# A gated linear attention and an MLP in one program: output products of 384 columns, two attention streams, whole padded loads, dummy products and a new order

## The chip, the cores and the metric

One core of one Trainium2 chip runs the program. The metric is device time in microseconds (us), the median of three runs: 546.33 before (545.84 to 546.39). The engines are named as in the profile: PE is TensorE's matmuls, PEld its weight loads, DVE VectorE, ACT ScalarE, POOL GpSimd, SP SyncE, which issues nearly all transfers.

## The reference

Four batches, 8 heads, 768 tokens, head size 48. The attention is a recurrence for each batch and head; its output, 3072 rows of 384, goes through an MLP with weights in float64:

```python
for t in range(S):
    state = alpha[:, :, t, :, None] * state + np.einsum('bhd,bhe->bhde', k[:, :, t], v[:, :, t])
    y[:, :, t] = np.einsum('bhd,bhde->bhe', q[:, :, t], state)
...
h = x @ w_in                                        # 384 -> 2048
sp = np.maximum(h, 0.0) + np.log1p(np.exp(-np.abs(h)))
return ((h * erf(sp)) @ w_out).astype(np.float32)   # 2048 -> 384
```

## The kernel before, in words

**Attention** is done in 24 chunks (class Chunk, line 251). A chunk is 64 tokens of two batches (m is the pair of batches, c the place in time), all 8 heads. la, lk, lq and lv load alpha, k, q and v. sb and sa are two scans of alpha on DVE; rc and ic note an inverse for a check at the end; kk and qq multiply k and q with the scans; pn turns K by PE and kn copies it out; ps makes the scores, mk masks them; qt and sv make the chunk's output in PSUM (py) from the state T and from the scores; pu and ta renew the state, td scales it. xh (ACT) and xl (DVE) split the output into a high and a low part, x_hi and x_lo, in the reduced float32 that PE multiplies fast. Chunks 0 to 11 are the first pair of batches in order of time, 12 to 23 the second.

**The MLP** is done in 12 blocks of 256 tokens (class Moe, line 418), two chunks each, in 4 groups g of 512 hidden units, and a group in two halves. hm (line 471) makes 18 products of 256 columns for a half, over x_hi, x_lo and the weights' parts wi_hi and wi_lo; he copies them out. u, n1, n2, n3, ma, mb, g, z1 and z2 are the activation, by two table sets on ACT: need (line 236) loads a set when the step wants another one than the last. ga and gl split the result into gh and gl; om (line 554) adds 18 products of 256 columns into acc: three blocks of 128 output columns, two of hidden units, three terms, with the weights as the stationary operand and the tokens as the columns. oe copies acc out three times, od sends it, oa on ACT's queue.

**Weights** come as float64, 12 blocks of w_in and 16 of w_out (class Weight, line 584). wl loads, wy, wv, wa and wb make float32 of the bits, wh the high part. The low part is made by wq (a subtraction on DVE) or by wp (two products on PE, with the identity and its negative) and we (a copy by ACT); before, all 12 blocks of w_in use wp and we, all 16 of w_out wq.

**The order** of all steps is a string, ORDER, read once (line 767). Class Queue (line 177) chains each engine's instructions in that order, SP's transfers too, so every engine works strictly through its part of the string. In the end f1, f2 and f3 reduce checks to one number, all engines load it, and a branch skips general (line 653), a slow path for unusual values that is not taken here.

Of the kernel before, what the change touches and what calls it, by code (L numbers as in the profile page):

```python
# [21 lines left out]
RT2 = 2.0**0.5  # L22
# [4 lines left out]
wli_0 wyi_0 wvi_0 wai_0 la_0 sb_0 rc_0 wli_7 wbi_0 whi_0 wpi_0 wli_9 lk_0 sa_0 wyi_7 wvi_7 wai_7 wyi_9 wli_5  # L27
la_1 lq_0 wvi_9 lv_0 wai_9 wli_1 wbi_7 wbi_9 kk_0 pn_0 wvi_5 lk_1 sb_1 whi_9 wpi_9 wyi_5 wai_5 wli_2 whi_7 wei_0
wpi_7 kn_0 qq_0 lv_1 ic_0 rc_1 sa_1 lq_1 la_2 wei_9 pu_0 ta_0 wyi_1 wvi_1 wei_7 wli_8 wyi_2 wli_6 wli_11 wbi_5
wli_3 wlo_0 ps_0 mk_0 sv_0 xh_0 wai_1 kk_1 pn_1 wli_4 wvi_2 wbi_1 wai_2 td_1 whi_5 whi_1 wpi_5 wbi_2 kn_1 wyi_8  # L30
wei_5 xl_0 pu_1 qq_1 ta_1 sb_2 wvi_8 wpi_1 qt_1 ps_1 td_2 wai_8 wvi_6 wbi_8 whi_2 lk_2 wyi_6 wpi_2 wei_1 mk_1
sv_1 wai_6 whi_8 wvi_11 ic_1 wyi_11 wei_2 xh_1 wbi_6 whi_6 wlo_7 wai_11 wvi_3 lq_2 wbi_11 wyi_3 wai_3 wpi_8
wei_8 whi_11 rc_2 ic_2 wpi_6 wei_6 wbi_3 sa_2 wli_10 whi_3 la_3 wyo_0 wpi_11 wei_11 xl_1 wvi_4 wpi_3 wei_3 wvo_0
wyi_4 wyo_7 kk_2 wao_0 wai_4 wvo_7 wbo_0 wlo_3 who_0 hm_0_0_0 he_0_0_0 wbi_4 whi_4 wao_7 wqo_0 pn_2 wbo_7 kn_2
hm_0_0_1 he_0_0_1 qq_2 wpi_4 wvi_10 lv_2 qt_2 sb_3 wyi_10 wai_10 wlo_5 rc_3 wlo_1 ps_2 mk_2 lk_3 wvo_3 wbi_10
wlo_2 wei_4 hm_0_1_0 pu_2 who_7 wqo_7 u_0_0 wyo_3 whi_10 wvo_5 he_0_1_0 wlo_6 sa_3 ta_2 la_4 n1_0_0 wvo_1 wao_3
wyo_5 sv_2 td_3 kk_3 wpi_10 wei_10 wbo_3 hm_0_2_0 wvo_2 who_3 wyo_2 wao_5 hm_0_1_1 pn_3 wyo_1 wqo_3 wao_2 xh_2
wao_1 he_0_2_0 lq_3 xl_2 hm_0_3_0 n2_0_0 wbo_1 n3_0_0 kn_3 lv_3 pu_3 lk_4 who_1 wbo_2 sb_4 ic_3 he_0_1_1 wlo_8
qq_3 qt_3 wbo_5 rc_4 who_2 wqo_1 ta_3 who_5 wqo_5 u_0_1 ma_0_0 g_0_0 he_0_3_0 ps_3 mk_3 td_4 hm_0_2_1 wlo_11
he_0_2_1 sv_3 kk_4 xh_3 wvo_6 n1_0_1 lq_4 sa_4 hm_0_3_1 la_5 xl_3 hm_1_0_0 he_0_3_1 mb_0_0 qq_4 n2_0_1 z1_0_0  # L40
wqo_2 z2_0_0 sb_5 pn_4 ic_4 n3_0_1 ma_0_1 kn_4 wyo_6 wvo_11 wvo_8 wao_6 lk_5 wlo_4 wlo_9 lv_4 ga_0_0_1 gl_0_0_1
hm_1_2_0 ga_0_0_0 qt_4 ps_4 mk_4 wbo_6 he_1_0_0 mb_0_1 he_1_2_0 kk_5 g_0_1 z1_0_1 gl_0_0_0 wyo_8 wao_8 who_6
u_0_2 n1_0_2 z2_0_1 hm_1_2_1 he_1_2_1 wyo_11 wao_11 wqo_6 wbo_8 rc_5 om_0_0_1 hm_1_1_0 he_1_1_0 pu_4 wvo_4
wbo_11 n2_0_2 n3_0_2 wyo_4 sv_4 who_11 ta_4 ma_0_2 wqo_11 om_0_0_0 ga_0_1_1 wao_4 wlo_10 xh_4 who_8 ic_5 td_5
wlo_12 pn_5 kn_5 hm_1_1_1 ga_0_1_0 wbo_4 who_4 wvo_9 wyo_9 mb_0_2 he_1_1_1 wao_9 xl_4 g_0_2 hm_1_0_1 wqo_8
gl_0_1_1 lv_5 hm_1_3_0 wqo_4 lk_6 wlo_13 he_1_0_1 he_1_3_0 om_0_1_1 sa_5 lq_5 wvo_10 wyo_10 hm_1_3_1 u_0_3
n1_0_3 z1_0_2 wao_10 qq_5 qt_5 ps_5 wyo_13 gl_0_1_0 wbo_9 who_9 n2_0_3 n3_0_3 z2_0_2 ga_0_2_0 om_0_1_0 la_6 lv_6
wqo_9 wyo_12 mk_5 ga_0_2_1 wbo_10 who_10 lq_6 sb_6 gl_0_2_0 wvo_13 ma_0_3 wqo_10 sv_5 xh_5 wvo_12 xl_5 g_0_3
wao_13 wao_12 u_1_0 he_1_3_1 wlo_15 gl_0_2_1 wlo_14 rc_6 u_1_1 n1_1_0 pu_5 ta_5 om_0_2_0 wvo_15 mb_0_3 wbo_13
n1_1_1 z1_0_3 wbo_12 hm_2_0_0 he_2_0_0 wyo_15 who_13 td_6 om_0_2_1 z2_0_3 sa_6 hm_2_1_0 he_2_1_0 kk_6 ga_0_3_0  # L50
# [36 lines left out]
xh_14 hm_6_1_0 he_6_1_0 u_5_3 om_5_0_0 sa_15 hm_6_1_1 n1_5_3 ga_5_1_0 n1_6_0 om_5_1_1 z2_5_2 hm_6_3_0 td_15
# [51 lines left out]

@with_exitstack  # L140
def gla_moe(ctx: ExitStack, tc: tile.TileContext, q, k, v, alpha, w_in, w_out, out):
    nc = tc.nc


    M, CPB, _, D, NP, NI, TC = q.shape
    P = NI * TC
    B, H, S = M * NI, 2 * NP, CPB * TC
    W = NP * NI * TC
    DM, NT = out.shape
    FF = w_in.shape[1]  # L150
    TB = 256
# [685 lines left out]
```

## Time and profile before

| | |
|---|---|
| median of 3 runs | 546.33 us |
| the profiled execution, own time | 547.01 us |
| its span, first to last instruction | 545.3 us |
| mean granted clock of TensorE | 0.995 |
| instructions | 18043 |
| PE / ACT / DVE busy | 516.9 / 496.2 / 470.5 us |
| ACT table loads | 64, 82.1 us |

The span is what the profiler sees of one execution; the execution's own time has 1.7 us more around it. "Busy" counts the time in which an engine had an instruction under way; ends of matmuls are modelled and overlap, so the distance of starts, not the length, is what one costs. All steps are recorded at line 185, the helper of class Queue, so the rows are told apart by tiles: `ph` is written by hm, `acc` by om, `py` by qt and sv, `pS` by ps, `rest` by wp, `wbuf` is a weight block being unpacked.

### The profile page before, as it was taken

To read this page: it belongs to the slowest core of one execution; us is meant where nothing else is said; L and a number is where in the kernel's file an instruction comes from. 1 tells how busy PE (TensorE), PEld (TensorE's weight loads), DVE (VectorE), ACT (ScalarE), POOL (GpSimd) and SP (SyncE) were. 2 spreads that over 40 slices of the span, in tenths; PEclk is the share of its full clock that TensorE was granted. 3 is DMA by queue.
4 is the path that set the end of the run, shared out by engine and by line. 5 is a ranking of instruction groups with operands and counts; after the bars stand their busy time and mean duration, and the time that the engine had idled before them with its cause. 6 is when DMAs were issued, how large, how long until landed. Compare 5 with 4: busy or idle time off the path is not lost.

```text
span 545.3 us, 18043 instructions
## 1 busy us (share of the span) xinstructions
PE 516.9 (95%) x7998; PEld 488.4 (90%) x7998; DVE 470.5 (86%) x613; ACT 496.2 (91%) x695; POOL 3.5 (1%) x18
## 2 busy tenths in 40 slices
PE   1799999999999999999999999999999999999984
PEld 0457999999999999999999999999999999999984
DVE  6899999999999999999698899698687887987772
ACT  3579999999999999898999999999899999999981
POOL 2000000000000000000000000000000000000000
PEclk9899999999999999999999999999999999999999
DMA  6967335213021023311022203022020202000001
GB/s 197 304 198 227 108 98 151 94 46 93 15 71 51 15 61 83 87 40 50 17 79 84 60 17 107 17 60 69 17 70 2 73 12 85 1 13 19 30 1 35
DMA packets 38101, 38.98 MB, mean 71 GB/s; under 512 B 22144, under 2 KB 26752, under 8 KB 38016
## 3 DMA queue, kind: packets, MB, share of 16 engines
q1 hardware_dynamic: 37872, 37.63, 23.6%
q8 instruction: 64, 1.05, 0.8%
q14 instruction: 21, 0.17, 0.1%
q10 hardware_dynamic: 144, 0.13, 0.1%
HBM read 33.03 MB, written 4.72 MB: 69 GB/s over the span
## 4 chain that ended last, share of the span: by engine, by line
PE 52%; ACT 35%; DVE 6%; issue 4%; DMA 1%; DVEq 0%; ACTq 0%; SPq 0%
PE ph L185 22%; PE acc L185 20%; ACT s L185 10%; ACT w L185 6%; ACT L185 6%; ACT gh L185 4%; ACT hs L185 4%; PE py L185 3%; PE rest L185 2%; DVE wbuf L185 2%; PE pu L185 2%; PE pS L185 2%; PE pn L185 1%; DMA raw_a<-in_alpha_dram 1%; ACT kn L185 1%
## 5 line engine op out<-in xcount | busy, mean ns | idle before, releaser
L185 PE MATMUL ph<-x_hi,wi_hi 128*128 128x256 f32 x576 | 165.5, 287 | 1.0 <-ACT hs L185 0.9
L185 PE MATMUL acc<-gh,wo_hi 128*128 128x256 f32 x576 | 164.9, 286 | 0.4 <-ACT gh L185 0.3
L185 PE MATMUL acc<-gl,wo_hi 128*128 128x256 f32 x576 | 162.7, 283 | 1.9 <-DVE gl L185 1.7
L185 PE MATMUL ph<-x_lo,wi_hi 128*128 128x256 f32 x576 | 162.0, 281 | 0.2 <-DVE x_lo L185 0.2
L185 PE MATMUL acc<-gh,wo_lo 128*128 128x256 f32 x576 | 161.8, 281 | 0.0
L185 PE MATMUL ph<-x_hi,wi_lo 128*128 128x256 f32 x576 | 161.7, 281 | 0.0
L185 PEld LDWEIGHTS ph<-x_hi,wi_hi 128*128 128x128 f32 x576 | 108.5, 188 | 4.0 <-ACT hs L185 1.6
L185 PEld LDWEIGHTS acc<-gl,wo_hi 128*128 128x128 f32 x576 | 108.5, 188 | 3.6 <-DVE gl L185 3.5
L185 PEld LDWEIGHTS acc<-gh,wo_hi 128*128 128x128 f32 x576 | 108.5, 188 | 2.5 <-ACT gh L185 0.7
L185 PEld LDWEIGHTS ph<-x_lo,wi_hi 128*128 128x128 f32 x576 | 108.6, 188 | 0.5 <-DVE x_lo L185 0.4
L185 PEld LDWEIGHTS acc<-gh,wo_lo 128*128 128x128 f32 x576 | 108.6, 188 | 0.0
L185 PEld LDWEIGHTS ph<-x_hi,wi_lo 128*128 128x128 f32 x576 | 108.5, 188 | 0.0
L185 DVE TENSOR_TENSOR gl<-hs,gh 128x512 fp32r<-128x512 f32 x96 | 65.3, 684 | 30.3 <-ACT gh L185 29.7
L185 ACT ACT_TABLE_LOAD x64 | 82.1, 1283 | 1.9 <-PEq L797 0.8
L185 ACT ACTIVATE gh<-hs 128x512 fp32r<-128x512 f32 x96 | 59.1, 624 | 9.5 <-PE acc L185 4.3
L185 DVE TENSOR_TENSOR t<-s,w 128x1024 f32<-128x1024 f32 x48 | 58.4, 1217 | 9.0 <-ACT w L185 8.7
L185 DVE TENSOR_TENSOR s<-s,w 128x1024 f32<-128x1024 f32 x48 | 58.5, 1219 | 8.9 <-ACT s L185 7.4
L185 DVE SCALAR_TENSOR_TENSOR hs<-s,hs 128x1024 f32<-128x1024 f32 x48 | 58.5, 1220 | 0.8
L185 DVE SCALAR_TENSOR_TENSOR w<-t,w 128x1024 f32<-128x1024 f32 x48 | 58.4, 1218 | 0.6
L185 ACT ACTIVATE hs<-ph 128x512 f32<-128x512 f32 x96 | 55.2, 587 | 1.7 <-PE ph L185 1.5
L185 ACT ACTIVATE s<-s,fixed 128x1024 f32<-128x1024 f32 x48 | 54.8, 1148 | 0.3
L185 ACT ACTIVATE s<-s 128x1024 f32<-128x1024 f32 x48 | 50.3, 1057 | 2.2 <-DVE t L185 1.8
(66 smaller groups left out, 637.9 us busy)
## 6 DMA issues: line engine op xcount, KB each, us to landing
wst<-in_moe_w_in_dram SPq DMA_DIRECT2D x12, 512.0 KB, 6.2
raw_v<-in_v_dram SPq DMA_DIRECT2D x24, 256.0 KB, 3.1
wst<-in_moe_w_out_dram SPq DMA_DIRECT2D x16, 384.0 KB, 4.0
raw_a<-in_alpha_dram SPq DMA_DIRECT2D x48, 96.0 KB, 2.9
raw_k<-in_k_dram SPq DMA_DIRECT2D x48, 96.0 KB, 2.6
raw_q<-in_q_dram SPq DMA_DIRECT2D x48, 96.0 KB, 2.3
out_dram<-o SPq DMA_DIRECT2D x35, 128.0 KB, 2.0
out_dram<-o ACTq DMA_DIRECT2D x1, 128.0 KB, 4.1
```

What stands on the lines that cost most here:

```text
L185: ins = made(*args, **kw)
```

## The change

- **om** takes the tokens as the stationary operand and 384 weight columns as the moving one: 12 products in place of 18. acc is two tiles of 128 tokens x 384. The terms run gh by wo_hi, gh by wo_lo, gl by wo_hi; in the last om of a block all of the first tile's products come first. hm runs x_hi by wi_hi, x_hi by wi_lo, then x_lo. The output is stored by tokens, in two transfers a block (od), without oa.
- **Chunks** alternate between the two pairs of batches (n = 2c + m), each with its own two T tiles. pn, ps, pu and f2 share one PSUM tile `both`, pu in columns 256 to 447 of either bank; a first product fills those columns. kn holds 48 of 64 columns, mask is BF16.
- **Loads** of alpha, k and q: the arrays are padded before the launch to 128 rows (alpha also between its segments), so one transfer brings a whole tile, and the memsets of these tiles go. k and q have two buffers each, and K and Q are formed in place.
- **Six blocks of w_in** (6 to 11) use wq in place of wp and we.
- **Dummy products** dw_n: n products of the identity with itself into acc's second bank, 57 in ten places of the order, 46 of them ahead of the first hm.
- **ORDER** is another. It begins with la_0, sb_0 and wlo_1. The steps u, g and n1, n2, n3 switch tables 59 times in the new string, 63 times in the old one. At the end ic_23 stands after the last om. The branch takes another layout.

The diff, cut to its core; of the order only the beginning and the end are shown:

```diff
-wli_0 wyi_0 wvi_0 wai_0 la_0 sb_0 rc_0 wli_7 wbi_0 whi_0 wpi_0 wli_9 lk_0 sa_0 wyi_7 wvi_7 wai_7 wyi_9 wli_5
+la_0 sb_0 wlo_1 wvo_1 rc_0 wyo_1 wao_1 sa_0 wbo_1 wli_1 wvi_1 wyi_1 who_1 wli_2 wli_5 wvi_2 wai_1 wyi_2 wai_2
+wqo_1 lk_0 wyi_5 wvi_5 wbi_1 whi_1 dw_22 wpi_1 la_1 kk_0 pn_0 wai_5 wbi_2 whi_2 wbi_5 whi_5 wli_0 wyi_0 wvi_0
...
-gl_11_2_0 om_11_2_0 z2_11_3 ga_11_3_1 gl_11_3_1 om_11_3_1 ga_11_3_0 gl_11_3_0 om_11_3_0 oe_11_2 od_11_2 f1 f2 f3
-oe_11_0 oe_11_1 oa_11_1 od_11_0
+z2_11_3 ga_11_3_0 gl_11_3_0 om_11_3_0 ga_11_3_1 gl_11_3_1 om_11_3_1 ic_23 oe_11_0 od_11_0 oe_11_1 f1 od_11_1 f2
+f3
...
-    rq, rk = (raw.tile([P, NP, NI, TC], F32, name=f"raw_{nm}") for nm in "qk")
-    for t, fill in ((ra, 1.0), (ra[:, 0 : 1 + L : SEG], 0.0), (rk, 0.0), (rq, 0.0)):
-        dve.memset(t, fill)
+    rq, rk = ([raw.tile([P, NP, NI, TC], F32, name=f"raw_{nm}{n}") for n in range(2)] for nm in "qk")
...
+    both = ps_at.tile([P, 2, 512], F32, name="both", tag="b")
...
-            self.m, self.c = divmod(n, CPB)
+            self.c, self.m = divmod(n, M)
...
         def lk(self):
-            self.load(rk.rearrange("p a i t -> p (a i) t"), k)
+            self.K = rk.pop(0)
+            rk.append(self.K)
+            sp.dma_start(out=self.K, in_=k[self.m, self.c])
...
         def hm(self, g, half):
-                for kt in range(KT):
-                    for wt, xt in ((wi_hi, x_hi), (wi_hi, x_lo), (wi_lo, x_hi)):
+            for wt, xt in ((wi_hi, x_hi), (wi_lo, x_hi), (wi_hi, x_lo)):
+                for u in range(2):
+                    for kt in range(KT):
...
         def om(self, g, half):
-            for d in range(KT):
-                for u in range(2):
-                    for n, (wt, gt) in enumerate(((wo_hi, gh), (wo_lo, gh), (wo_hi, gl))):
-                        pe.matmul(
-                            out=o, lhsT=wt[:, f, ds], rhs=gt[:, u, :],
...
+            terms = ((gh, wo_hi), (gh, wo_lo), (gl, wo_hi))
+            todo = [(c, u, n) for n in range(3) for c in range(TB // P) for u in range(2)]
+            if end:
+                todo.sort(key=lambda x: x[0])
+            for k, (c, u, n) in enumerate(todo):
+                gt, wt = terms[n]
+                pe.matmul(
+                    out=self.acc[c][:, :DM], lhsT=gt[:, u, c * P : (c + 1) * P], rhs=wt[:, g * GT + half * 2 + u, :],
+                    start=begin and (u, n) == (0, 0), stop=end and not any(c == x for x, *_ in todo[k + 1 :]),
+                )
...
-        def oe(self, d):
-            o = self.pl.gp.tile([P, TB], F32, name="o", tag="o", bufs=3)
+        def oe(self, c):
+            o = self.pl.gp.tile([P, DM], F32, name="o", tag=f"o{c}", bufs=1)
...
+        def dw(self, n):
+            for _ in range(n):
+                pe.matmul(out=self.t[:, :P], lhsT=ident, rhs=ident, start=True, stop=True)
...
-    with tc.If(rv > 0):
+    with tc.If(rv > 0, preferred_fallthrough_block=False):
```

## Rows read from the trace of the kernel before

**Rows 1.** The page's head: span, and each engine's busy time, share and instructions.
```profile
span 545.3 us, 18043 instructions
PE 516.9 (95%) x7998; PEld 488.4 (90%) x7998; DVE 470.5 (86%) x613; ACT 496.2 (91%) x695; POOL 3.5 (1%) x18
```

**Rows 2.** The table by stages: from and to, length, busy time and instructions of PE, PEld, DVE, ACT and POOL, then the granted clock of TensorE, the share of the DMA engines and GB/s.
```profile
20.00:39.28 19.28, 16.05 (x347) 9.09 (x346) 17.85 (x33) 12.80 (x27) 0.00 (x0) 0.91 0.79 252
39.28:100.00 60.72, 59.18 (x1111) 55.29 (x1114) 58.68 (x101) 58.09 (x91) 0.00 (x0) 1.00 0.50 147
100.00:220.00 120.00, 119.06 (x1957) 114.69 (x1945) 115.98 (x148) 118.44 (x166) 0.00 (x0) 1.00 0.20 55
220.00:380.00 160.00, 160.00 (x2511) 155.93 (x2510) 139.04 (x165) 151.99 (x207) 0.00 (x0) 1.00 0.21 57
380.00:500.00 120.00, 119.17 (x1798) 115.39 (x1797) 97.19 (x111) 115.58 (x153) 0.00 (x0) 1.00 0.12 33
500.00:537.80 37.80, 35.94 (x292) 34.59 (x291) 27.87 (x36) 30.28 (x39) 0.00 (x0) 1.00 0.03 11
```

**Rows 3.** The timeline of PE from 300 to 306 us, with one weight load (PEld) of the timeline of all engines: start, length, engine, line, operation and tiles.
```profile
300.47 0.28 PE L185 MATMUL ph<-x_hi,wi_lo 128*128 128x256 f32 x1
300.68 0.86 PE L185 MATMUL py<-Q,T 48*32 48x64 f32 x64
301.47 0.69 PE L185 MATMUL pS<-Q,K 48*64 48x64 f32 x32
302.09 0.39 PE L185 MATMUL acc<-gh,wo_hi 128*128 128x256 f32 x1
302.32 0.28 PE L185 MATMUL acc<-gh,wo_lo 128*128 128x256 f32 x1
302.32 0.19 PEld L185 LDWEIGHTS acc<-gl,wo_hi 128*128 128x128 f32 x1
304.21 0.27 PE L185 MATMUL acc<-gl,wo_hi 128*128 128x256 f32 x1
304.41 0.68 PE L185 MATMUL pu<-raw_v,kn 64*64 64x48 f32 x32
305.03 0.86 PE L185 MATMUL py<-sT,raw_v 64*32 64x64 f32 x64
305.81 0.38 PE L185 MATMUL ph<-x_hi,wi_hi 128*128 128x256 f32 x1
```

**Rows 4.** The timeline of PE ahead of the first product of the MLP; the second line is the second half of the pair in the first, seen in a narrower window.
```profile
36.98 1.02 PE L185 MATMUL rest<-wbuf,ident 128*128 128x512 f32 x2
37.41 0.59 PE L185 MATMUL rest<-wbuf,ident 128*128 128x512 f32 x1
38.07 1.02 PE L185 MATMUL rest<-wbuf,ident 128*128 128x512 f32 x2
39.28 0.39 PE L185 MATMUL ph<-x_hi,wi_hi 128*128 128x256 f32 x1
```

**Rows 5.** DVE up to 39.3 us: its first work on a weight block and its second x_lo in the timeline, and two lines of its waits (who, for whom: us in total, times, longest).
```profile
5.08 0.43 DVE L185 TENSOR_SCALAR wbuf<-wst 128x512 int32<-128x512 int32 x1 [2.38 <-DMA wst<-in_moe_w_in_dram]
38.60 0.53 DVE L185 TENSOR_TENSOR x_lo<-py,x_hi 128x384 fp32r<-128x384 f32 x1
DVE T L185 <- PE pu L185: 2.3, 2, 2.1
DVE B L185 <- DMA raw_a<-in_alpha_dram: 1.3, 1, 1.3
```

**Rows 6.** Groups of ACT's instructions by form, whole span: busy us, mean ns of one, and the idle time before them.
```profile
L185 ACT ACT_TABLE_LOAD x64 | 82.1, 1283 | 1.9 <-PEq L797 0.8
L185 ACT ACTIVATE wi_lo<-rest 128x512 fp32r<-128x512 f32 x12 | 7.1, 594 | 3.0 <-PE rest L185 2.9
L185 ACT ACTIVATE kn<-pn 128x512 f32<-128x512 f32 x22 | 12.9, 586 | 0.6 <-PE pn L185 0.6
L185 ACT ACTIVATE o<-acc 128x256 f32<-128x256 f32 x36 | 12.4, 376 | 4.2 <-PE acc L185 4.2
L185 ACT ACTIVATE x_hi<-py 128x384 fp32r<-128x384 f32 x24 | 11.5, 480 | 3.5 <-PE py L185 3.5
```

**Rows 7.** The end: the last PE product, the copies of acc, the last transfer issued (timelines), the time to landing of the last three output transfers (least, median, most), and two lines of PE's sequencer at the branch (length in ns, first and last start).
```profile
537.49 0.28 PE L185 MATMUL acc<-gl,wo_hi 128*128 128x256 f32 x1
537.81 0.94 ACT L185 ACTIVATE o<-acc 128x256 f32<-128x256 f32 x3 [4.17 <-PE acc L185]
538.77 0.38 ACTq L185 DMA_DIRECT2D out_dram<-o  x1
DMA to landing us min/median/max: 1.7/4.0/4.1
L782 PEldq COMPARE_BRANCH  x1: 4100/4100/4100, 538.7 to 538.7; - x1
L782 PEldq EVENT_SEMAPHORE  x1: 51/51/51, 542.9 to 542.9; - x1
```

**Rows 8.** A load of k in SP's timeline and its use by DVE, and the page's line on such loads (KB each, median us to landing).
```profile
291.79 0.80 SPq L185 DMA_DIRECT2D raw_k<-in_k_dram  x2
299.70 0.69 DVE L185 TENSOR_TENSOR K<-raw_k,B 128x512 f32<-128x512 f32 x1
raw_k<-in_k_dram SPq DMA_DIRECT2D x48, 96.0 KB, 2.6
```

More of the change, by code (lines that the diff above doesn't have):

```diff
@@ L142, in gla_moe @@
     nc = tc.nc
-    M, CPB, _, D, NP, NI, TC = q.shape
-    P = NI * TC
+    M, CPB, P, NP, NI, TC = q.shape
     B, H, S = M * NI, 2 * NP, CPB * TC
     W = NP * NI * TC
-    DM, NT = out.shape
+    NT, DM = out.shape
     FF = w_in.shape[1]
@@ L239, in need @@
             act.preload_act_table_set(name)
-    Ts = [at.tile([P, NI * NP * HD], F32, name="T", tag=f"T{n}", bufs=1) for n in range(2)]
-    for t in Ts:
+    Ts = [[at.tile([P, NI * NP * HD], F32, name="T", tag=f"T{m}{n}", bufs=1) for n in range(2)] for m in range(M)]
+    for t in Ts[0] + Ts[1]:
         nc.gpsimd.memset(t, 0.0)
-    T, Td = Ts
-    Tv, Tdv = (t.rearrange("p (i a d) -> p i a d", i=NI, a=NP)[:, :, :, :D] for t in Ts)
+    Tv = [[t.rearrange("p (i a d) -> p i a d", i=NI, a=NP)[:, :, :, :D] for t in pair] for pair in Ts]
+    both = ps_at.tile([P, 2, 512], F32, name="both", tag="b")
+    pe.matmul(
+        out=both[:, 1, NP * TC : NP * (TC + D)], lhsT=ident, rhs=Ts[0][0][:, : NP * D],
+        start=True, stop=True,
+    )
     PIECES = (((0, 0),), ((1, 16),), ((0, 32), (1, -16)))
@@ L312, in pn @@
                 return
-            self.pn_ = ps_at.tile([P, 2, 512], F32, name="pn", tag="b")
+            self.pn_ = both
             for pair in range(NP):
@@ L321, in kn @@
                 return
-            self.kn_ = at.tile([P, NP, 2, HD], F32, name="kn", tag="kn", bufs=1)
-            act.activation(self.kn_.rearrange("p a b d -> p (a b d)"), self.pn_[:, 0, :], AF.Copy)
+            self.kn_ = at.tile([P, NP, 2, D], F32, name="kn", tag="kn", bufs=1)
+            rows = self.pn_[:, 0, :].rearrange("p (a b d) -> p a b d", a=NP, b=2)
+            act.activation(self.kn_, rows[:, :, :, :D], AF.Copy)
         def td(self):
@@ L389, in pu @@
                 return
-            self.pu_ = ps_at.tile([P, NI, 512], F32, name="pu", tag="b")
+            self.pu_ = both[:, :, NP * TC :]
             for pair in range(NP):
@@ L395, in pu @@
                         pe.matmul(
-                            out=self.pu_[half * HD : (half + 1) * HD, i, pair * D : (pair + 1) * D],
+                            out=self.pu_[half * HD : half * HD + D, i, pair * D : (pair + 1) * D],
                             lhsT=self.kn_[toks, pair, half, :], rhs=self.v[toks, h * HD : h * HD + D],
@@ L658, in general @@
             DG = D // NG4
-            part = dram.tile([NG4, M, CPB, NI, TC, NP, 2, D], F32, name="part")
+            part = dram.tile([NG4, CPB, M, NI, TC, NP, 2, D], F32, name="part")
             rec = es.enter_context(ExitStack())
@@ L727, in general @@
                         m.om(g, half)
-                for d in range(KT):
+                for d in range(2):
                     m.oe(d)
@@ L757, in f2 @@
         def f2(self):
-            self.pf = ps_at.tile([P, 2, 512], F32, name="pf", tag="b")
+            self.pf = both
             pe.matmul(out=self.pf[:1, 0, :1], lhsT=self.good[:, 3:4], rhs=ones, start=True, stop=True)
@@ L765, in gla_moe, with __init__ @@
     flags = Flags()
+    class Warm:
+        def __init__(self):
+            self.t = None
+        def dw(self, n):
+            if self.t is None:
+                self.t = ps_acc.tile([P, 512], F32, name="warm", tag="acc1")
+            for _ in range(n):
+                pe.matmul(out=self.t[:, :P], lhsT=ident, rhs=ident, start=True, stop=True)
+    warm = Warm()
     for name, arg in steps:
@@ L820 @@
             a[..., 1, :] = a[:, :, ::-1, :, :, 1, :].copy()
+            wide = _np.full((M, C, 2, 64, NP, NI, TC), float(name == "alpha"), a.dtype)
+            wide[:, :, :, :D] = a
+            a = wide.reshape(M, C, 128, NP, NI, TC)
+            if name == "alpha":
+                wide = _np.zeros((M, C, 128, 1 + NP * NI * (TC + 1)), a.dtype)
+                wide[..., 1:].reshape(M, C, 128, NP, NI, TC + 1)[..., :TC] = a
+                a = wide
         elif name == "moe_w_in":
```

302 lines of the change are left out of this document (144 added, 158 removed).

## The prediction

> **What bounds the kernel now.** I read the engines' shares first [rows 1]: TensorE (PE) 95%, ScalarE (ACT) 91%, VectorE (DVE) 86%. Three engines that full hide who leads, so the table by stage comes next [rows 2]. From the first product of the MLP at 39.28 us [rows 4] on, PE is busy in nearly all of each stage, ACT in 474.4 of 498.5 us, and DVE in 174.7 of the 180.7 us up to 220 and much less later. But a PE that looks busy need not be dense, so the PE timeline is my price list [rows 3]. Inside a group the starts of two products of 256 columns lie (304.21 - 302.32) / 16 = 0.118 us apart, 2.126 us for 18. A visit to the attention costs 0.79 for qt, 0.62 for ps, 0.62 for pu and 0.78 for sv, plus 0.2 for going and coming back: 0.09 before the first py product and 0.11 because the first acc product takes 0.23. pn is put at 0.43, four times 128 columns at the fp32 rate below.
>
> Now the sum behind the first product: 192 groups x 2.126 = 408.2; 21 qt, 22 ps, 20 pu, 22 sv and 20 pn = 68.4; 63 visits (counted in the order string) x 0.2 = 12.6; one split of a weight block 1.1. That is 490.3 of the 498.3 us from 39.28 to the end of the last product at 537.6 (start 537.49, [rows 7]). So PE's own work sets the end; only 8 us are lost, and a shorter product is worth its whole saving until ACT or DVE take over. Ahead of the first product DVE leads: it does 50 steps (counted in the order string), then x_lo of the second chunk at 38.60; it waits 2.38 us for the first weight block, 1.3 for alpha and 2.3 for PE's pu [rows 5]. PE's granted clock is lowered for part of it (0.91 as the mean of 20 to 39.28 us, 1.00 in every later stage [rows 2]).
>
> **The change part by part.**
> Output products. 18 products of 256 columns per group become 12 of 384: the same 4608 columns, a third fewer instructions. No row shows a slot of 384. At one column a cycle of 2.4 GHz, 256 columns would take 106.7 ns; the rows show 118. Is the rest a price per column, per product, or a weight load that 256 columns just fail to cover? The nearest rows: a 512-column fp32 product starts 36.98, its second half 37.41 [rows 4], 0.43 later, where streaming at two cycles a column is 0.427: hardly anything is added when the stream is long. A weight load starts with each product (302.32 [rows 3]) for the next one, and 384 columns give it 53 ns more time. So I take 160 + 2.3 = 162.3 ns, 1.95 a group, 0.178 saved x 96 = **17.1 us**. Ends: the same 11 ns added (171.4 ns) leaves 6.6 us; scaled by columns (177 ns), nothing.
> The Trainium skill, TensorE: Matmul & The Clock Gate, section Back-to-back issue gap, gives N/2.4 + 2.5 ns for a product alone, at full clock: 109.2 for 256 and 162.5 for 384. By it a group would go from 1.966 to 1.950 and the change of shape would be worth 1.5 us in all; but the rows show 118 for 256, not 109, so the trace does not bear it out where it can be tried.
>
> Order within a group. gl and x_lo come last now: eight of twelve output products and twelve of eighteen input products run without them. Price nothing; it shortens waits that PE hardly has in the middle, and a little in the last 38 us, where 1.9 us of PE stand idle [rows 2].
>
> Attention. PE issues the same products. kn copies 384 columns instead of 512 (0.59 to 0.48 by x_hi, a PSUM copy of 384 [rows 6]), 2.3 us of ACT. T alternates between two sets, which only loosens a chain. pS, pu and pn share one tile with fixed places, so pu need not wait for sT. K and Q are formed in place: at no cost in DVE time, but the load of k now waits for ps and pn of two chunks before (rival three). Behind the first product one pu and one qt more remain: 0.6 + 0.8.
>
> Loads. One issue in place of two for alpha, k and q; four memsets leave DVE at the start, two join POOL, which has nothing to do later. Alpha's load is first on SP's queue, ahead of the weight blocks, and wlo_1 goes ahead of the input blocks. So DVE can scan at about 4 us, where it began with a weight block at 5.08 and then waited 1.3 for alpha [rows 5].
>
> Weights. Six of twelve lower halves go from PE (1.09 us, the distance 36.98 to 38.07 [rows 4]) and ACT (0.59 [rows 6]) to one DVE subtraction. Five of these six PE splits lay ahead of the first product, one (1.1) behind.
>
> Dummies. 57, each two passes of 128 columns of fp32: 2 x 0.107 = 0.215 (a quarter of 0.43). 46 stand ahead of the first product, in PE's waits there; if these waits are shorter than thought they delay it, at most 46 x 0.215 = 9.9, at half clock twice that. 11 stand behind it: 2.4 us, paid in full where PE is dense.
>
> First product. DVE does 50 steps ahead of the second x_lo in both. Off go the later start (1.1), part of the waits for the load (1.0) and for a slow pu (1.0), and x_lo is no longer needed at the group's start (0.7): **35.5** in place of 39.28, between 33 and 39.3.
>
> ACT. The order asks for 59 table switches, not 63: 4 x 1.283 = 5.1. With kn, wi_lo (two fewer behind the first product, 1.2) and 24 copies of acc at 0.48 in place of 36 at 0.38 it has about 465 us left behind the first product. At the 483.9 below that is 96%, before 95%. DVE gains 3 subtractions and the scans, td and ta that moved behind, some 5 us. I charge **3 us** for the closer race.
>
> End. From 537.6 to 545.3 are 7.7 us. Two things end together at 542.9 [rows 7]: the last output transfer (issued 538.77, 4.1 to land) and PE's branch over the unused path (538.7, 4100 ns). The change takes both: the branch no longer jumps, and the first half of the tokens is copied and sent while PE does the second, so one copy (0.48) and one transfer are left. I put landing at 2.8, between 1.7 and 4.1: 1.7 us less; bounds 0 (either one stays) and 2.8. The flags now wait for ic_23, which stands at the end of ACT's queue: 0.2 us, behind the last products; only the two copies queue behind it.
>
> **Sum** against the profiled execution. 498.3 - 17.1 - 1.1 + 1.4 + 2.4 = 483.9 from first to last product, + 3 = 486.9; from 35.5 to 522.4; + 6.0 = 528.4 of span (545.3 before). The execution's own time is 1.7 above its span (547.01), and the median 0.7 below that: 528.4 + 1.7 - 0.7 = **529.4**.
>
> **Rivals.**
> One: the long product saves little. Same 11 ns added: 10.5 worse, 539.9. A cost by columns: 546.5. For it: no row of 384; against it: the pair in [rows 4].
> By the formula of the Trainium skill quoted above it would be 529.4 + 15.6 = 545.0; the trace's 118 ns speak against it, and it gets 0.02.
> Two: DVE or ACT becomes the bound while weights are still unpacked. Up to 220 us DVE has only 6.0 us and ACT 4.2 us free [rows 2]; the order puts 5 us more on DVE there and takes 4 to 5 from PE. If the idle stays as it is, this stage ends 7 to 10 us later than by PE's sum, 3 of which are charged: 533 to 537. Against it: the order is another, and idle that comes from PE shrinks with PE.
> Three, slower: SP's queue. A load of k waits until pn and ps of two chunks before have read the buffer, and alpha, v, weights and outputs queue behind it. Now it is issued at 291.79, lands in 2.6 and is used at 299.70 [rows 8]: 5.3 us to spare. If the wait eats more than that, every chunk holds PE: 6.1 us of delay would cost 0.8 x 22 = 17.6 and undo all; 7 us gives 22 x 1.7 = 37, so 567. Against it: in the order string pn stands well ahead of the load that needs its buffer.
> The dummies may not lift the clock: then the first product stays at 39.3, 533, within the forecast's own spread.
>
> **How the numbers follow.** Forecast, 522 to 534: 0.64. Better, as with DVE starting early and PE losing less than 8: 0.05. Rival one 0.11: 0.07 with the same 11 ns added, 0.04 near 546. Rival two 0.15. Rival three 0.05. What one can tell from no change here is about 0.2%, 545.2 to 547.4. Faster: 0.64 + 0.05 + 0.07 + 0.15 + 0.01 = 0.92; same 0.03; slower 0.05. The range 520 to 541 takes in rival two and the milder half of rival one, and leaves out some 0.04 below and 0.12 above.
>
> **What would show it.** Right: acc products of 384 columns about 162 ns apart; first ph product at 33 to 38; PE still dense to the end, 60 table loads; no 4 us branch on PE after the last product, and an end about 6 us after it. Wrong: 171 ns or more between acc products; DVE over 98% busy from 40 to 220 with PE below 97%; DVE waits that name raw_k or raw_a after 60 us; a tail of 7.7 us as before.

## The result, and the profile after

| | before | after |
|---|---|---|
| median of 4 runs, us | 546.36 (545.84 to 548.03) | 532.32 (531.97 to 532.62) |
| ratio | | 0.9738, 95% interval 0.9716 to 0.9759 |
| profiled execution: own time / span | 547.01 / 545.3 | 531.97 / 530.2 |
| first product of the MLP | 39.28 | 31.68 |
| last product started on PE | 537.73 | 523.45 |

14.0 us came off; 529.4 was forecast, 520 to 541 the range. The sum was close by luck: most of its largest term was not there, and a part priced at nothing turned out to hold up the rest.

The head of the page after, to be read beside [rows 1]:

```profile
span 530.2 us, 16957 instructions
PE 513.2 (97%) x7520; PEld 488.0 (92%) x7520; DVE 470.0 (89%) x615; ACT 484.3 (91%) x673; POOL 4.4 (1%) x20
```

PE has 478 instructions fewer (the output products alone are 576 fewer), but only 3.7 us less busy time. ACT loads a table set 60 times, as forecast (64 before). The table by stages, columns as in [rows 2]:

```profile
20.00:31.68 11.68, 10.67 (x243) 8.35 (x242) 11.63 (x23) 6.42 (x14) 0.00 (x0) 1.00 0.71 270
31.68:60.00 28.32, 27.92 (x563) 26.03 (x562) 28.32 (x50) 26.34 (x43) 0.00 (x0) 1.00 0.45 146
60.00:100.00 40.00, 39.24 (x628) 36.59 (x627) 39.90 (x66) 38.61 (x59) 0.00 (x0) 1.00 0.46 145
100.00:220.00 120.00, 118.74 (x1861) 113.57 (x1860) 115.08 (x147) 117.06 (x165) 0.00 (x0) 1.00 0.21 64
220.00:380.00 160.00, 159.67 (x2444) 153.97 (x2443) 140.22 (x167) 150.78 (x200) 0.00 (x0) 1.00 0.22 66
380.00:500.00 120.00, 119.86 (x1561) 116.65 (x1560) 99.42 (x114) 116.57 (x153) 0.00 (x0) 1.00 0.13 40
```

The granted clock is 1.00 from 20 us to the first product too (0.91 before), DVE is full from 20 to 100 us, and PE stays dense to the end. Then PE's timeline in the middle, the counterpart of [rows 3]:

```profile
302.57 0.87 PE L184 MATMUL ph<-x_hi,wi_lo 128*128 128x256 f32 x6
303.28 0.87 PE L184 MATMUL ph<-x_lo,wi_hi 128*128 128x256 f32 x6
...
306.47 0.95 PE L184 MATMUL acc<-wo_hi,gh 128*128 128x384 f32 x4
307.26 0.87 PE L184 MATMUL acc<-wo_lo,gh 128*128 128x384 f32 x4
307.97 0.87 PE L184 MATMUL acc<-wo_hi,gl 128*128 128x384 f32 x4
```

Six products of 256 columns take 0.71 us, 0.118 each as before. Four of 384 take 0.71 too (307.26 to 307.97): 0.177 each in this row, 174.7 ns as the mean over all groups. I had taken 162.3.

Taking the distance of starts as what a product costs, and adding it up by kind from the first product to the last (oldterms is an experiment below):

| us on PE, by starts | before | after | oldterms |
|---|---|---|---|
| ph (hm) | 212.8 | 211.1 | 218.0 |
| acc (om) | 214.5 | 210.8 | 218.7 |
| pn / qt / pS / sv | 7.2 / 17.0 / 13.8 / 18.6 | 8.3 / 17.3 / 13.6 / 18.0 | 8.4 / 17.3 / 13.2 / 17.4 |
| pu | 12.2 | 9.1 | 8.8 |
| rest (wp) / dummies | 2.4 / 0 | 0 / 3.4 | 0 / 3.1 |
| sum | 498.4 | 491.8 | 504.9 |
| of ph and acc, above their plain slots (waits, coming and going) | 18.5 | 16.3 | 31.2 |

So of the 15.1 us of span 7.6 went ahead of the first product, 6.7 in the stream, and 0.8 in the tail (7.6 to 6.8, from the last start on PE to the end).

The start, beside [rows 4, 5]: PE, then DVE's first work and its two waits up to 33.7 us.

```profile
31.68 0.95 PE L184 MATMUL ph<-x_hi,wi_hi 128*128 128x256 f32 x6
32.47 0.87 PE L184 MATMUL ph<-x_hi,wi_lo 128*128 128x256 f32 x6
33.60 0.99 PE L184 MATMUL ph<-x_lo,wi_hi 128*128 128x256 f32 x6 [0.26 <-DVE x_lo L184]
```
```profile
3.67 1.24 DVE L184 TENSOR_TENSOR_SCAN B<-raw_a,back 128x520 f32<-128x520 f32 x1 [3.67 <-DMA raw_a<-in_alpha_dram]
33.00 0.55 DVE L184 TENSOR_TENSOR x_lo<-py,x_hi 128x384 fp32r<-128x384 f32 x1
```
```profile
DVE B L184 <- DMA raw_a<-in_alpha_dram: 3.7, 1, 3.7
DVE wbuf L184 <- DMA wst<-in_moe_w_in_dram: 0.9, 1, 0.9
```

Up to the second x_lo DVE starts 1.4 us earlier (5.08 to 3.67), waits 0.9 behind that instead of some 4.2, and has 0.8 us less to do; and PE begins 1.3 us ahead of that x_lo, where it had begun 0.7 behind its start. 1.4 + 3.3 + 0.8 + 2.0 is the 7.6 found, to a tenth.

The end, beside [rows 7]: the last pair of om's products, the last copy, and the branch on PE's sequencer (length in ns: least, median, most; first and last start).

```profile
522.99 0.51 PE L184 MATMUL acc<-wo_hi,gl 128*128 128x384 f32 x2
523.53 0.49 ACT L184 ACTIVATE o<-acc 128x384 f32<-128x384 f32 x1 [0.55 <-PE acc L184]
L788 PEldq COMPARE_BRANCH  x2: 95/2118/4140, 524.5 to 524.8; - x2
```

PE's jump is still there, 4.14 us from 524.8. SP, which waits for the outputs, is through its semaphores at 526.2 and its own branches at 526.3.

### The profile page after: what moved, and what is told of

Same layout as the page of the kernel before. It is cut to its first block, busy times and chain, and to the rows that moved or that the text cites. A ratio compares the mean times of both kernels' runs of the same rounds, so it can differ in the third digit from the quotient of the medians.

```text
span 530.2 us, 16957 instructions
## 1 busy us (share of the span) xinstructions
PE 513.2 (97%) x7520; PEld 488.0 (92%) x7520; DVE 470.0 (89%) x615; ACT 484.3 (91%) x673; POOL 4.4 (1%) x20
## 4 chain that ended last, share of the span: by engine, by line
PE 51%; ACT 20%; DVE 19%; issue 6%; DMA 3%; SPq 0%; DVEq 0%; ACTq 0%
PE acc L184 22%; PE ph L184 22%; ACT s L184 6%; ACT w L184 4%; PE py L184 4%; DVE wbuf L184 3%; PE both L184 3%; ACT L184 3%; ACT gh L184 2%; DVE t L184 2%; DVE s L184 2%; ACT hs L184 2%; DVE w L184 2%; DVE hs L184 2%; DVE gl L184 2%
## 5 line engine op out<-in xcount | busy, mean ns | idle before, releaser
L184 PE MATMUL acc<-wo_hi,gh 128*128 128x384 f32 x384 | 88.4, 347 | 1.3 <-ACT gh L184 1.3
L184 PE MATMUL ph<-x_hi,wi_hi 128*128 128x256 f32 x576 | 86.8, 286 | 0.5 <-ACT x_hi L184 0.4
L184 PE MATMUL acc<-wo_hi,gl 128*128 128x384 f32 x384 | 85.1, 338 | 0.8 <-DVE gl L184 0.8
L184 PE MATMUL acc<-wo_lo,gh 128*128 128x384 f32 x384 | 84.6, 337 | 0.0
L184 PE MATMUL ph<-x_lo,wi_hi 128*128 128x256 f32 x576 | 83.9, 281 | 0.4 <-DVE x_lo L184 0.3
L184 PE MATMUL ph<-x_hi,wi_lo 128*128 128x256 f32 x576 | 83.7, 281 | 0.0
L184 PEld LDWEIGHTS ph<-x_lo,wi_hi 128*128 128x128 f32 x576 | 74.8, 188 | 1.0 <-DVE x_lo L184 1.0
L184 PEld LDWEIGHTS acc<-wo_hi,gl 128*128 128x128 f32 x384 | 68.1, 188 | 2.0 <-DVE gl L184 1.7
L184 PEld LDWEIGHTS acc<-wo_hi,gh 128*128 128x128 f32 x384 | 64.6, 188 | 4.3 <-ACT gh L184 2.3
L184 PEld LDWEIGHTS acc<-wo_lo,gh 128*128 128x128 f32 x384 | 68.5, 188 | 0.0
```

Of the source, the lines that this page charges most:

```text
L184: ins = made(*args, **kw)
```

## The experiments

"Control" is the changed kernel again. Each group shares its runs of the kernel before: 546.83 us for control, om256, kn64 and nolate, 546.53 for noif and the two nosign kernels, 546.44 for the rest. The last two columns are of the profiled execution.

| kernel | median, us | ratio to before, 95% interval | first product | last start on PE |
|---|---|---|---|---|
| control | 531.80 | 0.9725 (0.9712 to 0.9739) | 31.75 | 523.71 |
| om256 | 532.51 | 0.9744 (0.9731 to 0.9757) | 31.31 | 524.00 |
| kn64 | 532.88 | 0.9746 (0.9733 to 0.9759) | 31.50 | 523.55 |
| nolate | 532.91 | 0.9746 (0.9730 to 0.9763) | 31.68 | 523.96 |
| noif | 529.39 | 0.9682 (0.9668 to 0.9696) | 33.03 | 524.40 |
| nosign | 531.49 | 0.9725 (0.9710 to 0.9739) | 31.27 | 523.08 |
| nosign_nolate | 532.13 | 0.9730 (0.9716 to 0.9744) | 31.21 | 521.96 |
| b_om384 | 545.08 | 0.9973 (0.9955 to 0.9991) | 39.12 | 535.55 |
| noearly | 535.55 | 0.9791 (0.9766 to 0.9815) | 33.17 | 527.83 |
| alast | 535.60 | 0.9803 (0.9790 to 0.9817) | 34.80 | 525.95 |
| oldterms | 544.75 | 0.9971 (0.9958 to 0.9983) | 31.64 | 536.51 |

**after_again.** 

> The changed kernel as it is, the control for the three beside it. All theories: 532.3 us, between 531.5 and 533.0, 0.974 of the kernel before.

It came as expected.

**om256: the shape of the output products alone, undone.**

```diff
-out=self.acc[c][:, :DM], lhsT=gt[:, u, c * P : (c + 1) * P], rhs=wt[:, g * GT + half * 2 + u, :],
+out=self.acc_of(d), lhsT=wt[:, g * GT + half * 2 + u, d * P : (d + 1) * P], rhs=gt[:, u, :],
```

> The output products alone go back: weights stationary, 18 products of 256 columns a group, three copies and three transfers a block; the order and all else as changed. Theory A, a PE product costs nearly by its columns: the trace of after has 174.7 ns a slot of 384 and 118.25 of 256, so a group gets 18 x 118.25 - 12 x 174.7 = 32 ns longer, x 96 = 3.1 us: 535.4 us, and with one more copy and transfer at the end 535 to 537. Theory B, the one I had predicted by (a long product streams at 162 ns and something else in the new kernel cost 14 us): undoing it costs 17 us, about 549. Rival C, the long slots bought nothing, and the gain of the slots is eaten by waits in either form: 532 +- 0.7.

0.7 us between the medians, and the intervals overlap. acc takes 212.4 us by starts, the control 210.7: 1.8, where the slots alone say 3.1; the longer products waited 1.3 us more around their groups. B is out: no 14 us hide in the new kernel. By the time C is met (532 +- 0.7) and A is not (535 and more); on PE a good half of A's 3.1 us is there.

**b_om384: the same change alone, in the kernel before.**

```diff
-out=o, lhsT=wt[:, f, ds], rhs=gt[:, u, :],
+out=self.acc[c][:, :DM], lhsT=gt[:, u, c * P : (c + 1) * P], rhs=wt[:, f, :],
```

> The kernel before, with the output products alone changed to 12 of 384 columns (terms still within each block of hidden units, output by tokens in two transfers a block, the causal mask in BF16 to make room). Theory A, cost by the column: (18 x 118.25 - 12 x 174.7) ns x 96 = 3.1 us less PE, all of it on the path since PE sets the end there: 543 to 544.5 against 546.8 (ratio 0.994). Theory B, the waits around the groups eat it as they seem to do in the changed kernel: 546 to 547. The prediction's price (162.3 ns) would give 529.7.

1.4 us by the medians, 0.5 to 2.5 by the interval, between A and B; 2.0 in the stream of the profiled execution (498.4 to 496.4). The shape is worth 0.7 us in the new kernel and 1.4 in the old one by the medians, about 2 in either on PE, not 17.

**widths: why 174.7 ns.**

```python
for i in range(48):
    nc.tensor.matmul(out=t[:m, :w], lhsT=src[:, i % 2, (i % 3) * 128 : (i % 3) * 128 + m], rhs=src[:, 2 + i % 2, :w], ...)
```

> A kernel that leaves out the whole computation: chains of 48 products on an otherwise idle chip, behind 40 products that warm the clock; each chain with another number of columns. r: reduced float32, stationary operand 128 columns wide; n: the same with 32 columns; b: bfloat16 with 128. Theory A, a cost by the column in the stream of the moving operand: r256 118, r384 175, r512 232 ns a product, n the same, the line through them about 0.44 ns a column with some 5 ns a product. Theory B, the one I had predicted by (about 0.417 ns a column and a fixed 2 to 11 ns, the 118 being an edge where the weight load does not fit behind the product): r384 162, r512 216, and n256 below r256 since its load is short. Theory C, the other engines' traffic in the full kernel stretches the stream: here r256 near 109 and r384 near 163. b is there to tell whether four-byte operands are what costs: by A's reason b256 near 109, b384 near 162.

PE alone, by windows inside one chain each: r384, then b384. Columns: from and to, length, busy time and instructions, granted clock, DMA share, GB/s.

```profile
36.00:43.00 7.00, 7.00 (x43) 1.00 0.00 0
96.00:103.00 7.00, 7.00 (x45) 1.00 0.01 2
```

The counts take in the product under way at either edge; the mean distances of the starts, a chain's first two left out, are sharper:

| ns a product | 256 | 320 | 384 | 448 | 512 |
|---|---|---|---|---|---|
| reduced float32, 128 wide | 119.9 | 146.7 | 173.4 | 206.7 | 227.4 |
| the same, 32 wide | 117.8 | | 173.6 | | 231.6 |
| bfloat16, 128 wide | 109.2 | | 162.5 | | 215.8 |

B's 162 and 216 are out (173 and 227), and so is C: without the other engines 256 columns still take 118 to 120. A weight load of 32 columns is shorter (108 ns by the mean of its group, 193 with 128 columns), yet it moves the slot by no more than -2.1, 0.2 and 4.2 ns, so the weight load made next to nothing of the 118. A's numbers (118, 175 and 232) are met within 2%, but its reason, a cost by the column, is not shown. bfloat16's rows lie 0.417 ns a column apart. What reduced float32 takes above that bare time is 13.2, 13.4 and 14.1 ns at 256, 384 and 512 columns with the 128-wide operand that the kernel uses, nearly the same for every product (20.0 at 448), and 11.1, 13.6 and 18.3 with the 32-wide one, growing with the columns. The kernel's own rows lie midway: from 118.25 at 256 columns, the same excess would give 171.6 at 384, scaling by columns 177.4, and 174.7 was measured.

bfloat16 alone follows 0.417 a column and 2.5 a product. The formula quoted in the prediction from the Trainium skill, TensorE: Matmul & The Clock Gate, section Back-to-back issue gap, agrees with that to 0.1 ns in all three widths; for reduced float32 it is 9 to 18 ns low.

**kn64: pu's stationary operand wide again.**

```diff
-out=self.pu_[half * HD : half * HD + D, i, pair * D : (pair + 1) * D],
-lhsT=self.kn_[toks, pair, half, :], rhs=self.v[toks, h * HD : h * HD + D],
+out=self.pu_[half * HD : half * HD + wide, i, pair * D : (pair + 1) * D],
+lhsT=self.kn_.rearrange("p a b d -> p (a b d)")[toks, at0 : at0 + wide], rhs=self.v[toks, h * HD : h * HD + D],
```

> kn's part in the products of pu (the stationary operand) is 64 columns wide again for 14 of the 16 products of a chunk, in place of 48; the same number of products, all else as changed. In the trace of after a visit to pu takes 0.434 us, before 0.611, which I had priced at nothing. Theory A, the narrow stationary operand makes the pair cheaper (21 visits, 0.177 each, 14 of 16 of it): +3.2 us, 535.5. Theory B, pu got cheaper by the new places of its output in PSUM or by the order of its products: 532.3, within 0.5, and the visit stays at 0.43.

Groups of pu's products by form: before, then in kn64 (busy us, mean ns of one, idle time).

```profile
L185 PE MATMUL pu<-raw_v,kn 64*64 64x48 f32 x704 | 15.0, 223 | 0.0
```
```profile
L184 PE MATMUL both<-raw_v,kn 64*64 64x48 f32 x616 | 14.7, 224 | 0.0
L184 PE MATMUL both<-raw_v,kn 64*48 64x48 f32 x88 | 5.7, 206 | 0.0
```

The mean is 224 ns in both where 64 are given, and 206 with 48. By starts a visit takes 0.523 us, against 0.434 in the control and 0.611 before: 0.09 of the 0.177 is the width (0.155 was expected of 14 products in 16), and what the rest is wasn't tried. So A is right in kind and about half in size. Of 1.9 us more on PE none reached the last start (0.15 earlier, with a start 0.25 earlier); the medians lie 1.1 apart with overlapping intervals.

**nolate: no dummies behind the first product.**

```diff
-mk_3 z1_0_0 lv_3 rc_4 dw_5 sv_3 ta_2 xh_3 xl_3 wbo_2 td_4 z2_0_0 ...
-ma_0_1 dw_2 hm_1_0_0 ... la_5 dw_4 qt_4
+mk_3 z1_0_0 lv_3 rc_4 sv_3 ta_2 xh_3 xl_3 wbo_2 td_4 z2_0_0 ...
+ma_0_1 hm_1_0_0 ... la_5 qt_4
```

> Without the 11 dummy products behind the first product of the MLP; the 46 ahead of it stay. Theory A, PE is dense there and each pair is paid in full, 22 starts that took 3.4 us in the trace of after: 529.0, between 528.5 and 530. Theory B, they stand in waits of PE that come back as idle time: 532.3, within 0.6. Theory C, they keep the granted clock up there, and without them it falls below 1.00 between 32 and 100 us: slower than 533.

The stages of nolate, columns as in [rows 2]:

```profile
31.68:60.00 28.32, 25.95 (x544) 24.31 (x543) 28.32 (x50) 26.34 (x43) 0.00 (x0) 0.97 0.46 149
60.00:100.00 40.00, 38.74 (x620) 36.28 (x620) 39.34 (x64) 37.57 (x57) 0.00 (x0) 0.98 0.46 145
```

PE's idle grows by 2.0 and 0.5 us, DVE is as full as before up to 60 us and 0.6 us less full behind it, and the clock falls to 0.97 and 0.98. That is B with C's sign: 3.4 us of work went and nothing was gained; 1.1 us slower by the medians, within the intervals.

**nosign, and nosign_nolate: is it DVE that binds there?** Both leave out 16 steps on DVE; the second also the late dummies.

```diff
-... wbi_11 ... wbo_4 ... wbo_6 ... wbo_14        (16 wb steps behind the first hm)
```

> Leaves out 16 of DVE's weight steps behind the first product (wb, which puts the sign bit into a weight block, one of 512 and 15 of 384 columns): 0.68 + 15 x 0.53 = 8.6 us less on DVE between 31 and 220 us, nothing else changed. Theory A, DVE is the bound from 31 to 140 us (busy 108.7 of 109 us in the trace of the control, PE idle 1.8 us there): PE takes up the idle, 1 to 2.5 us faster than 531.8. Theory B, PE binds there too: 531.8 +- 0.6. Theory C, ACT binds from 100 on (39.82 of 40): a gain up to 100 us is given back by 140, 531.8 +- 0.6 with an earlier first output product.

> The same 16 DVE steps left out, and the 11 dummies behind the first product too. Leaving out the dummies alone gave 0 to +1 us. Theory A, DVE was what kept those 3.4 us of PE from counting: now they count, 3 to 4 us less than with the 16 steps alone, 526 to 528.5. Theory B, ACT is what keeps them from counting: no faster than with the steps alone. Theory C, the lower clock (0.98 without the dummies) eats them: PE dense but slots longer up to 100 us.

With 8.6 us less on DVE the first output product comes 1.4 us earlier (73.41 to 71.97) and the last start 0.6; with the dummies out too, 2.6 and 1.7. The medians show neither (531.49 and 532.13). Product for product nosign leads the control by 1.5 us at 140 us, still 1.4 at 369 us and 0.6 at the end, so C's reason, that ACT takes the gain back by 140, isn't borne out either. Still DVE's 108.71 of 109 us from 31 to 140 were no bound worth 8.6: in nosign DVE has 102.81 there, and PE went only from 107.20 to 107.69. The next limit is 1.8 us away on PE itself, and from 100 to 140 ACT is busy 39.80 to 39.82 of 40 us with and without the steps. My A for nosign_nolate, 3 to 4 us, is not borne out; the profiled executions show 1.1, and that of nosign_nolate is the fastest of its five.

**noif: the end.**

```diff
-    with tc.If(rv > 0, preferred_fallthrough_block=False):
-        general()
```

> The branch at the end and the slow path that it skips are left out; the flags are still reduced and loaded by all engines. Theory A, PE's jump of 4.14 us alone sets the end in the trace of after (last output landed near 525.9, jump over at 528.97): the end comes near 526 to 527.2 in place of 530.2, the time 3 us lower, 528.8 +- 0.6. Theory B, the closing of the program waits for something else (landing, the drains of the queues) that ends with it: 531.8 +- 0.7. If my prediction's reason (landing 2.8 after the last copy) held, 529.5.

2.4 us faster by the medians (0.9 to 3.9 by the ends of the two intervals). In the profile the span ends 527.9 - 524.40 = 3.5 us behind the last start on PE, in the control 530.5 - 523.71 = 6.8. A holds: the jump alone is the last 3.3 us. This execution ended its PE stream 0.7 us later than the control's, so 2.6 of them came off its span.

The Trainium skill, Runtime: NRT & Kernel Launch, section Instruction fetch mechanics, says that a taken branch to a place not yet fetched stalls the engine until it is. The traces agree as far as they go: behind 524 us the DMA queues of the kernel after carry instructions (packets, MB, share of 16 engines), and from 524.7 us to its end noif has none. That the 4.14 us are spent waiting for these is not shown.

```profile
q14 instruction: 6, 0.05, 2.8%
q8 instruction: 2, 0.03, 2.7%
```

**noearly: no dummies ahead of the first product.**

```diff
-... whi_1 dw_22 wpi_1 ... lq_0 qq_0 dw_2 ps_0 ... whi_7 ... (46 in seven places)
+... whi_1 wpi_1 ... lq_0 qq_0 ps_0 ...
```

> Without the 46 dummies ahead of the first product of the MLP; the 11 behind it stay. Theory A, they hold PE's granted clock at 1.00 up to there and so shorten the attention's PE steps that DVE waits for: clock about 0.9 from 20 us, first product 1 to 2 us later, 533 to 534. Theory B, DVE leads the start whatever PE's clock is: first product at 31.7, 531.8 +- 0.7. Theory C, they stand in the way of PE's real work: earlier and faster.

Its stages ahead of the first product, then PE at 290 us (timeline) and the windows there, PE's busy time alone and the clock:

```profile
20.00:31.00 11.00, 6.65 (x137) 3.50 (x135) 10.95 (x22) 5.93 (x12) 0.00 (x0) 0.80 0.69 257
31.00:33.17 2.17, 2.17 (x70) 1.69 (x69) 2.17 (x4) 1.26 (x4) 0.00 (x0) 0.50 1.06 342
```
```profile
290.45 0.45 PE L179 MATMUL acc<-wo_hi,gh 128*128 128x384 f32 x1
293.12 1.12 PE L179 MATMUL acc<-wo_hi,gh 128*128 128x384 f32 x3 [2.23 <-issue]
294.04 1.48 PE L179 MATMUL acc<-wo_lo,gh 128*128 128x384 f32 x4
295.32 1.28 PE L179 MATMUL acc<-wo_hi,gl 128*128 128x384 f32 x4
```
```profile
290.45:293.12 2.67, 0.45 (x8) 0.94 0.53 191
293.12:296.44 3.32, 3.32 (x12) 0.53 0.02 5
296.44:297.50 1.06, 1.06 (x11) 1.00 0.00 0
```

A holds for the clock (0.80, then 0.50) and the first product, 1.4 us later, but not for its reason: DVE waits no longer than before (its second x_lo starts at 33.31, in the control at 33.34). It is PE's own steps that the lower clock stretches. noif, which keeps the dummies, shows the same: behind a wait of 1.86 us its clock is 0.58 for 3.1 us, and its first product comes at 33.03 (PE's timeline, then that window).

```profile
27.23 0.69 PE L184 MATMUL both<-raw_q,raw_k 48*64 48x64 f32 x32 [1.86 <-DVE raw_k L184]
33.03 0.96 PE L184 MATMUL ph<-x_hi,wi_hi 128*128 128x256 f32 x6
```
```profile
28.71:31.82 3.11, 3.11 (x68) 0.58 0.82 294
```

But the output product that comes at 284.01 us in the control comes at 284.26 in noearly: all but 0.3 was made up for. What makes this execution slow is a stall of 2.2 us in which PE waited for nothing that the profile shows, and the clock behind it. The five runs spread from 532.77 to 536.8, so such a stall may come and go; a transfer of instructions lies in the hole, but the control has one at the same place without a stall. The cause, and whether the dummies have to do with it, stays open.

**alast: alpha's first load fourth in the queue.**

```diff
-la_0 sb_0 wlo_1 wvo_1 rc_0 wyo_1 wao_1 sa_0 wbo_1 wli_1 wvi_1 wyi_1 who_1 wli_2 wli_5
+wlo_1 wvo_1 wyo_1 wao_1 wbo_1 wli_1 wvi_1 wyi_1 who_1 wli_2 la_0 sb_0 rc_0 sa_0 wli_5
```

> The first load of alpha goes fourth on SP's queue, behind three weight blocks, and its scans, reciprocal and check note go behind DVE's first weight steps; all else as changed. Theory A, DVE's chain ahead of the first product sets the start and its beginning is what alpha's early load bought: DVE starts at about 4.8 in place of 3.67 and waits for alpha again, first product 1 to 2.5 us later, and the end by the same, 533 to 534.5. Theory B, an early loss is made up for behind it: 531.8 +- 0.7, whatever the first product does.

DVE in its first 9 us:

```profile
3.98 0.52 DVE L179 TENSOR_SCALAR wbuf<-wst 128x384 int32<-128x384 int32 x1 [3.98 <-DMA wst<-in_moe_w_out_dram]
...
7.73 1.24 DVE L179 TENSOR_TENSOR_SCAN B<-raw_a,back 128x520 f32<-128x520 f32 x1 [1.63 <-DMA raw_a<-in_alpha_dram]
```

The scan starts 4.1 us later than in the trace of after (3.9 than in the control) and the first product 3.0 later, more than I expected; 2.2 of it is left at the last start on PE, and the medians differ by 3.8 (the profiled execution is the fastest of its five). A holds: an early loss on DVE's chain is carried to the end, where noearly's, on PE's clock, was made up for.

**oldterms: the order within the groups, undone.**

```diff
-for wt, xt in ((wi_hi, x_hi), (wi_lo, x_hi), (wi_hi, x_lo)):
-    for u in range(2):
-        for kt in range(KT):
+for u in range(2):
+    for kt in range(KT):
+        for wt, xt in ((wi_hi, x_hi), (wi_hi, x_lo), (wi_lo, x_hi)):
...
-todo = [(c, u, n) for n in range(3) for c in range(TB // P) for u in range(2)]
+todo = [(c, u, n) for c in range(TB // P) for u in range(2) for n in range(3)]
```

> The order within the groups of products goes back (hm: by block and by input rows, the x_lo term second; om: all of a token block and a hidden block together, the gl term third of six), shapes and the order of the steps as changed. The prediction priced it at nothing behind the first product and 0.7 us at it. Theory A: the second product of the first group needs x_lo, which comes at 33.5 us in the control, 1.8 us behind the first product: +1.8 us there, and some 0.1 us more waiting for gl and x_lo in every few groups: 533.5 to 536. Theory B, the loss at the first group is made up for: 531.8 +- 0.7.

13 us slower than the control by the medians, far outside either theory, and within 0.2 to 0.4% of the kernel before. PE's two leading waits over the whole span (us in total, times, longest) in oldterms, the same in the control, and one of them in oldterms' timeline:

```profile
PE acc L184 <- DVE gl L184: 5.4, 10, 0.8
PE ph L184 <- DVE x_lo L184: 5.1, 7, 1.6
```
```profile
PE acc L184 <- DVE gl L184: 0.8, 2, 0.5
...
PE ph L184 <- DVE x_lo L184: 0.5, 1, 0.5
```
```profile
267.82 0.28 PE L184 MATMUL ph<-x_hi,wi_hi 128*128 128x256 f32 x1
268.87 0.38 PE L184 MATMUL ph<-x_lo,wi_hi 128*128 128x256 f32 x1 [0.77 <-DVE x_lo L184]
```

One product of the group has run and the next needs x_lo. With the lows last, 12 x 0.118 = 1.4 us of hm and 8 x 0.175 = 1.4 us of om run first; with the lows second and third, 0.12 and 0.35. The new order string places xl and gl that close to the products. These two waits are 9.2 of the 14.9 us by which ph and acc grew above their plain slots; a granted clock of 0.97 and 0.98 from 60 to 140 us is part of the rest. hm and om were not undone apart.

## Why the prediction was right or wrong

**Output products: mis-sized.** The step said 162.3 ns and 17.1 us; 174.7 ns and, by slots, 3.1 us is what came, 0.7 to 1.4 in the time; 171 ns or more was the sign it had named against itself. The anchor was at fault: the second half of a 512-column fp32 pair [rows 4] is another kind of stream, and its 0.43 said nothing of reduced float32. The nearest row was the 256-column product of the same type [rows 3]: with its 11 ns kept it gave 171.4, by columns 177, and 174.7 lies midway between these two ends, which had 0.11 together. Rival one was the case, between its two halves, and on its own would have put the time at 529.4 + 17.1 - 3.1 = 543.4. (The 0.02 for the formula must lie within rival one's 0.04 near 546, or the chances come to more than 1.)

**What hid the error** was luck, and not one thing. Predicted against measured, in us of span: first product -3.8 / -7.6; om -17.1 / -3.7, waits around its groups included; wp -1.1 / -2.4 (two blocks, not one); pu and qt +1.4 / -2.8; dummies +2.4 / +3.4; race +3 / 0; pn, pS, sv and ph 0 / -1.3; tail -1.7 / -0.8. Together -16.9 / -15.1. Gains that were not priced, or not in full, stand in for the 13.4 us that om did not bring.

**Order within a group: the step that failed worst,** though it shows nowhere in that list. "Price nothing" was read from the waits of the old string, in which PE waited 1.7 us for gl (us in total, times, longest):

```profile
PE acc L185 <- DVE gl L185: 1.7, 4, 1.1
```

It is the new string that needs it: without it 31.2 us instead of 16.3 go above the plain slots, and nearly all of the gain is gone. So the gain belongs to the string and the term order together. What the term order would bring in the old string was not tried.

**First product.** Right in kind, half in size, and below the 33 us named as the least: alpha's early landing, fewer DVE waits and a late x_lo, all three as named. alast shows that the first is real and reaches the end; the other two are read from the traces and were not undone by themselves. I had charged 1.0 + 1.0 for waits of which 3.3 went, 0.7 for an x_lo that frees 2.0, and nothing for 0.8 us less work on DVE.

**Attention.** "PE issues the same products" missed that pu would come 3.1 us cheaper on PE. kn64, with 14 of 16 products wide again, gives back 1.9 of it on PE, so that much is kn's 48 columns; the rest was not tried, and the time shows 1.1 us, within the intervals.

**Dummies.** Ahead of the first product they lift the clock, which the prediction left open; but without them it comes at 33.2, not at the 39.3 that it feared. Behind it, 2.4 us was too low (3.4) and "paid in full" was wrong: nolate got none of the 3.4 us back.

**DVE or ACT (rival two).** The sign it named, DVE over 98% from 40 to 220 us with PE below 97%, is there for DVE up to 100 us alone (115.08 of 120 behind that, 96%), and PE stays at 98% and more. Relief of DVE by 8.6 us bought 0.3 us by the medians and 0.6 at the last start: PE stood 1.8 us behind it.

**SP's queue (rival three).** The sign was there, the harm was not. DVE's waits after 60 us name both loads (us in total, times, longest):

```profile
DVE B L184 <- DMA raw_a<-in_alpha_dram: 2.1, 2, 1.6
...
DVE raw_k L184 <- DMA raw_k<-in_k_dram: 1.0, 1, 1.0
```

3 us in all, on an engine with 11% to spare; PE's stages above have no room for 17 us, the price at which this rival would have decided.

**Tail.** The branch still jumps; the layout moved it. The outputs were quicker than assumed, 1.8 to 1.9 us to land in place of 2.8 (least, median, most below), and noif shows that they would have been enough.

```profile
DMA to landing us min/median/max: 1.8/1.8/1.9
```

## What to carry to other kernels

Before a wider product is priced, take the slot from a product of the same type in the same stream, and both ways, with its excess kept and scaled by columns: here 171.4 and 177 held the 174.7 between them, and a product of another type gave 162. Where an order of steps and an order of terms are changed together, the one can spend the slack that the other gives: price them as a pair, by how much PE work stands ahead of the first use of a late operand. And in a stage that two or three engines fill, a saving on one of them was worth no more than the free time of the next.

## What the runs showed of the hardware

On an idle chip, with a stationary operand of 128 columns, reduced float32 took 119.9, 146.7, 173.4, 206.7 and 227.4 ns a product for 256 to 512 columns in steps of 64, which is 13 to 14 ns above 0.417 ns a column but for 20 at 448; bfloat16 took 2.5 above it. A product of 48 columns took 224 ns by the profile's mean with a stationary operand 64 columns wide and 206 with 48. A hole of 2.2 us in a dense PE stream was followed by 3.3 us at a granted clock of 0.53: products of 384 columns then took 1.28 / 4 = 0.32 us, the time of 384 columns at 1.2 GHz. By starts the hole cost 2.5 us and the clock behind it about another 1.4. A wait of 1.86 us in noif was followed by 1.5 us at 1.00 and then 3.1 us at 0.58.
